# Weight units stored with their sums and loaded into the place of their smaller parts, operands prepared a chunk ahead, and a last chunk that hands its places over

## The chip, the cores and the metric

One core of one Trainium2 chip. Five engines work side by side and wait for each other through semaphores: TensorE (PE in the profile, its weight loads PEld), VectorE (DVE), ScalarE (ACT), GpSimd (POOL) and SyncE (SP), which here issues most of the DMAs. The metric is the device time of one execution in microseconds, the median of the runs. Everything is float32; each large product is made from a larger and a smaller part of each operand (`hi` and `lo`, in the format float32r), as three products of the parts.

## The reference

Random-feature attention over 8 batches of 8 heads with 576 positions of 64 values and 128 features, whose result, as 4608 rows of 512 values, goes through a gated layer of 1536 columns.

```python
def phi(x):
    proj = np.einsum('bhsd,md->bhsm', x, omega)
    h = proj - np.sum(x * x, axis=-1, keepdims=True) / 2.0
    h = h - np.max(h, axis=-1, keepdims=True)
    return np.exp(h) / np.sqrt(m)
q_p, k_p = phi(q * scale), phi(k * scale)
kv = np.einsum('bhsm,bhsd->bhmd', k_p, v)
num = np.einsum('bhsm,bhmd->bhsd', q_p, kv)
den = np.einsum('bhsm,bhm->bhs', q_p, np.sum(k_p, axis=2))[..., None] + 1e-06
x = (num / den).transpose(0, 2, 1, 3).reshape(4608, 512)
gate = 1.0 / (1.0 + np.exp(-(x @ w_gate)))
out = (gate * (x @ w_val)) @ w_out
```

The three weight matrices arrive as float64 and are converted on the chip.

## The kernel before

The work has four stages on TensorE.

1. **Attention**, in small steps (norms of rows `ss`, keys up to `kv`, queries up to `xs`), each with projections `pp`, maxima `mx`, exponentials, and for queries transposes `pt` and products `pn` and `px`. The finished columns `xs` go to the scratch `xT` in HBM. A generator interleaves the steps of several tasks.
2. **First pass**: four of the twelve column tiles of the gated layer, with plain products `gv` (line 225, 12 matmuls of 128x512 for gate and for value) over chunks of 512 rows of `xT`. A chunk's rows are loaded into `xr` and split into operands `xe` (ScalarE copies, GpSimd subtracts, line 70). Its results `ye` go to HBM. It starts as soon as the first rows of `xT` are there: one step of it, then fourteen small steps of attention (`RATE`), so that both share TensorE until attention ends; what remains of it then is its end.
3. **Second pass**: the other eight column tiles as four pairs, for nine chunks, by a scheme with 7 products in place of 8 (`gated`, products `gw`, line 320, 42 matmuls of 128x256 in each of 72 groups; a group belongs to a chunk, a pair and a kind, gate or value). Its results `yl` go to HBM.
4. **Third pass** (`last`, products `po`, line 416): for each of 18 half chunks 6 steps j of 21 matmuls with the output weights; its rows `yr` come back from `ye` and `yl` and are split into `yh` and `yl`.

Weights of the second and third pass form 14 units: 0 to 7 for the second, 8 to 13 for the third. Each comes as four blocks of 128x256 (1 MB as float64). A "piece" is half of it, 512 columns: `from_float64` takes six VectorE instructions (lines 78 to 94) and an add on GpSimd (line 96). The four converted blocks are kept in HBM (`w32`). Later `unit` loads them, makes four sums of blocks on VectorE (line 192) and splits the seven operands into a larger part (ScalarE, 128x768 and 128x1024) and a smaller part (VectorE). Eight units are converted beside attention, one piece every second step of the first pass (`PUT`), and six in the first pass's end.

A unit's parts lie in a place `u`, of which `late` has five and `tail` three. The pools: `early` holds the first pass's weights and closes with it; `a` is attention's and closes with attention; `late` opens then in the same memory; `tail` opens in place of `early`. Tiles of one tag share its places in turn, and an instruction that would overwrite a place waits for its last reader. In the last chunk units 8 to 13 are loaded through a single place, `xr` (named `wbt`).

A scheduler orders the instructions of each engine; those wrapped in `pin` keep the order in which they are written. Within an engine everything runs in order, so a waiting instruction holds up what stands behind it.

Of the kernel before, what the change touches and what calls it, by code (L numbers as in the profile page):

```python
# [48 lines left out]
PUT = 2  # L49
# [23 lines left out]
def from_float64(nc, both, bits, n):  # L73
# [3 lines left out]
    a, t = both[:, :n], both[:, n:]  # L77
# [19 lines left out]
    return x  # L97
# [3 lines left out]
def attn_glu_kernel(ctx: ExitStack, tc, qT, kT, qn, kn, va, om, ident, w, out):  # L101
# [6 lines left out]
    w32 = dram.tile([N_LATE, P, 4, Q], F32, name="w32")  # L108
# [30 lines left out]
    def piece(tiles, i):  # L139

        raw = tiles("wraw", i, 2 * WP).rearrange("p (n two) -> p n two", two=2)
        nc.sync.dma_start(out=raw, in_=w[:, i * WP : (i + 1) * WP, :])
        return from_float64(nc, tiles("f64", i, 2 * WP), raw, WP)

    def first_weights(pool, tiles):

        n = WE // WP
        for j in range(NE):
            ws[j] = wh, wl = [pool.tile([P, WE], F32R, name=f"{t}{j}") for t in ("wh", "wl")]
            for i in range(n):  # L150
                s = slice(i * WP, (i + 1) * WP)
                split(nc, wh[:, s], wl[:, s], piece(tiles, j * n + i), lo_engine=nc.gpsimd)
                yield

    def convert_weights(tiles, ns):

        flat = w32.rearrange("n p b q -> n p (b q)")
        k = 4 * Q // WP
        for n in ns:
            for i in range(k):  # L160
                x = piece(tiles, NE * WE // WP + n * k + i)
                nc.sync.dma_start(out=flat[n, :, i * WP : (i + 1) * WP], in_=x)
                yield

# [9 lines left out]
    def unit(pool, n, at=None):  # L174

        if at is None:
            both = keep.tile([P, KC, NC], F32, tag="xr", bufs=1, name=f"wbt{n}")
            b, t = both[:, :2], both[:, 2:]
        else:
            b, t = (buffer(f"{x}{n}", F32, at) for x in ("wb", "wt"))  # L180
        b, t = (x.rearrange("p a (b q) -> p (a b) q", q=Q) for x in (b, t))
        nc.sync.dma_start(out=b, in_=w32[n])
        yield
        u = pool.tile([P, 2, N_OPS, Q], F32R, tag="u", bufs=UL if pool is late else UE, name=f"u{n}")
        units[n] = u[:, 0], u[:, 1]
        for o, x, y in (
            (t[:, 0], b[:, 3], b[:, 0]),
            (t[:, 2], b[:, 2], b[:, 3]),
            (t[:, 1], b[:, 2], t[:, 0]),
            (t[:, 3], b[:, 1], t[:, 1]),  # L190
        ):
            nc.vector.tensor_tensor(out=o, in0=x, in1=y, op=ALU.subtract)
        split(nc, u[:, 0, :3], u[:, 1, :3], b[:, :3])
        split(nc, u[:, 0, 3:], u[:, 1, 3:], t)
        yield
# [10 lines left out]
    def first_pass():  # L206


        def parts_of(o, n):
            raw = load(o, n)  # L210
            yield
            for k in range(KC):
                x = buffer(f"xe{o}_{k}", at=keep)[:, :, :n]
# [17 lines left out]
        x = [t for t in parts_of(*chunks[0]) if t is not None]  # L231
        for (o, n), after in zip(chunks, chunks[1:] + [None]):
            ahead, parts = [], iter(())
            for j in range(NE):
                if j == NE - 1 and after:
                    parts = parts_of(*after)
                    next(parts)
# [4 lines left out]
                yield  # L242
                val = product(1, j, o, n, x)
# [7 lines left out]
            x = ahead + [t for t in parts if t is not None]  # L251
# [50 lines left out]
    def gated(c, x, pair, kind, g, y):  # L302
# [57 lines left out]
        pin(nc.sync.dma_start(out=yl[pair - EP, :, c], in_=y))  # L360

    def second_pass(x, parts):


        held = iter(())
        for c in range(NCH):
            ahead = None
            for pair in range(EP, NPAIR):
                g = keep.tile([P, 4, 2, P], F32, tag="g", bufs=2, name=f"gl{pair}_{c}")
                y = keep.tile([P, 2, N_OPS, P], F32, tag="y", bufs=2, name=f"yl{pair}_{c}")  # L370
                for kind in range(2):
# [12 lines left out]
                    yield c, pair  # L384
            x = ahead
        next(held, None)

    def last(c, s):
# [8 lines left out]
        for j in range(NPAIR):  # L397
            t, n = (("y", 2 * N_OPS), ("g", 8))[j % 2]
            raw = keep.tile([P, n, P], F32, tag=t, bufs=2, name=f"yr{id_}_{j}")[:, :8]
            if j < EP:  # L400
                nc.sync.dma_start(out=raw[:, :2], in_=ye[j, :, c, :, 0, s])
                nc.sync.dma_start(out=raw[:, 2], in_=ye[j, :, c, 1, 1, s])
                nc.sync.dma_start(out=raw[:, 7], in_=ye[j, :, c, 0, 1, s])
                for o, a, b, op in ((3, 7, 2, ALU.add), (4, 3, 0, ALU.subtract), (5, 0, 7, ALU.subtract), (6, 1, 4, ALU.subtract)):
                    nc.vector.tensor_tensor(out=raw[:, o], in0=raw[:, a], in1=raw[:, b], op=op)  # L405
            else:
                nc.sync.dma_start(out=raw[:, :N_OPS], in_=yl[j - EP, :, c, s])
# [95 lines left out]
    def keys(pool, u, p, b):  # L503
# [37 lines left out]
        kv = pool.tile([P, 2, E], F32, tag="kv", bufs=16, name=f"kv{u}_{p}_{b}")  # L541
# [4 lines left out]
    def queries(pool, u, p, b):  # L546
        for g in projected(pool, "q", u, p, b, qT):
# [54 lines left out]
            xs = pool.tile([P, nt * P], F32, tag="xs", bufs=XS, name=f"xs{id_}")  # L602
# [47 lines left out]
    keep = ctx.enter_context(tc.tile_pool(name="keep", bufs=1))  # L650
    with tc.tile_pool(name="early", bufs=1) as early:
        gates = first_pass()
        with tc.tile_pool(name="a", bufs=1, side="right") as pool:
            steps = attention(pool)

            def tiles(tag, i, n):
                return pool.tile([P, n], U32, tag=tag, bufs=2, name=f"{tag}{i}")
# [10 lines left out]
            later = convert_weights(tiles, range(UL + UE))  # L668
            n = credit = 0
            while not ready(B * S):  # L670
# [6 lines left out]
                if next(conv, conv) is conv and n % PUT == 0:  # L677
                    next(later, None)
# [3 lines left out]

        left = 2 * NE * (NCH + 1) - n

        def tiles(tag, i, n):
            return buffer(f"{tag}{i}", U32, late).rearrange("p a b -> p (a b)")

        conv = convert_weights(tiles, range(UL + UE, N_LATE))
        parts = iter(())
        for n, _ in enumerate(gates):  # L690
            if n < left - 2 * NE - 2:
                next(conv, None)
# [32 lines left out]
    for one in started:  # L725
        next(one)
# [76 lines left out]
```

## Time and profile before

| | |
|---|---|
| median of 3 runs | 1288.71 us (1285.23 to 1290.4) |
| the profiled execution's own time | 1282.94 us |
| its span | 1281.1 us |
| mean granted TensorE clock | 0.954 |
| TensorE busy in matmuls | 1176.0 us (92%) |
| VectorE busy | 904.7 us (71%) |
| attention and most of the first pass | 0 to 511.6 us |
| end of the first pass | to 584.4 us |
| second pass's products | 588.8 to 989.7 us |
| third pass | from 999.3 us to the end |

The profile's windows give, for a stretch of the span, the busy time of each engine and the number of its instructions, then TensorE's granted clock as a share of full speed and the busy share of the DMA engines. The waits give, for an engine and line, the time that it stood idle and the instruction that released it. The chain goes back from the last instruction through what released each. Instructions of tiles have the tile's name without its number; a line number is that of the kernel listed above.

### The profile page before, as it was taken

Reading aid. Unit: us, or ns where it says so; the run is one execution under the profiler, and the core shown is the slowest. Engines: PE = TensorE matmul, PEld = TensorE weight load, DVE = VectorE, ACT = ScalarE, POOL = GpSimd, SP = SyncE. Lnnn points to the kernel's source line nnn. Section 1 sums busy time; section 2 is a strip of 40 time slices with the busy share of each in tenths; the row PEclk is TensorE's granted clock in tenths of the full one; section 3 lists DMA queues with packets and bytes.
Section 4 is the critical chain, followed back from the end, with each engine's and each line's share of the span. In section 5 each row is a group of like instructions: output and inputs, shape, how many; then the busy total and the mean of one; then the engine's idle time right before and its main releaser. Section 6 shows DMA issues by size and latency. Waiting matters only on the chain.

```text
span 1281.1 us, 24183 instructions
## 1 busy us (share of the span) xinstructions
PE 1176.0 (92%) x8828; PEld 1110.7 (87%) x8828; DVE 904.7 (71%) x2057; ACT 604.7 (47%) x1222; POOL 496.8 (39%) x545
## 2 busy tenths in 40 slices
PE   5779989999999999883999999999996799999998
PEld 5768979788979888762899999999996799999998
DVE  7788988886676755778765665656656777777774
ACT  5557777778767674213422322223223444344331
POOL 3544452534142421332466666667643211111120
PEclk8869989999999999996999999999997799999999
DMA  7665778766534502675133233322333666666663
GB/s 260 209 192 161 213 230 269 222 210 185 177 93 119 165 32 90 194 227 171 63 143 110 98 120 138 131 109 98 120 120 124 204 204 205 200 188 190 182 185 104
DMA packets 104950, 206.58 MB, mean 161 GB/s; under 512 B 11136, under 2 KB 42112, under 8 KB 104832
## 3 DMA queue, kind: packets, MB, share of 16 engines
q1 hardware_dynamic: 87984, 186.09, 45.9%
q10 hardware_dynamic: 16848, 18.95, 4.3%
q8 instruction: 70, 1.15, 0.4%
q14 instruction: 48, 0.39, 0.1%
HBM read 136.31 MB, written 68.68 MB: 160 GB/s over the span
## 4 chain that ended last, share of the span: by engine, by line
PE 73%; DVE 13%; DMA 6%; issue 3%; ACT 2%; POOL 1%; SPq 1%; ACTq 0%; DVEq 0%; POOLq 0%
PE gw L320 26%; PE po L416 21%; PE gv L225 8%; PE pkv L537 5%; PE pnq L580 5%; PE ptq L568 2%; DMA wraw<-w 2%; DVE mxq L494 1%; DMA wbt<-w 1%; PE ppq L489 1%; DVE hq L557 1%; DVE mxk L494 1%; PE ppk L489 1%; PE pxq L597 1%; PE ppq L491 1%
## 5 line engine op out<-in xcount | busy, mean ns | idle before, releaser
L320 PE MATMUL gw<-xl,u 128*128 128x256 f32 x3024 | 373.2, 286 | 32.4 <-ACT p L331 19.6
L320 PEld LDWEIGHTS gw<-xl,u 128*128 128x128 f32 x3024 | 370.1, 194 | 35.7 <-ACT p L331 20.5
L416 PE MATMUL po<-u,yh 128*128 128x256 f32 x1512 | 273.6, 284 | 0.0
L416 PEld LDWEIGHTS po<-u,yh 128*128 128x128 f32 x1512 | 235.9, 191 | 0.0
L416 PE MATMUL po<-u,yl 128*128 128x256 f32 x756 | 214.7, 284 | 12.1 <-DVE yl L70 12.1
L225 PE MATMUL gv<-xe,wh 128*128 128x512 f32 (+1 forms) x640 | 198.9, 386 | 7.5 <-POOL xe L70 6.3
L69 ACT ACTIVATE yh<-yr 128x896 fp32r<-128x896 f32 x108 | 100.6, 950 | 162.3 <-PE po L416 72.8
L416 PEld LDWEIGHTS po<-u,yl 128*128 128x128 f32 x756 | 145.0, 192 | 12.5 <-issue 9.5
L225 PEld LDWEIGHTS gv<-xe,wh 128*128 128x128 f32 x640 | 115.8, 194 | 26.0 <-POOL xe L70 10.7
L225 PE MATMUL gv<-xe,wl 128*128 128x512 f32 (+1 forms) x320 | 124.4, 390 | 9.3 <-DVE ye L245 4.1
L70 POOL TENSOR_TENSOR yl<-yr,yh 128x896 fp32r<-128x896 f32 x18 | 41.1, 2281 | 221.9 <-PE po L416 151.9
L70 DVE TENSOR_TENSOR yl<-yr,yh 128x896 fp32r<-128x896 f32 x90 | 97.4, 1090 | 37.9 <-PE po L416 26.3
L70 POOL TENSOR_TENSOR loq<-rawq,hiq 128x256 fp32r<-128x256 f32 (+1 forms) x80 | 55.3, 704 | 126.2 <-ACT hiq L69 120.6
L300 DVE TENSOR_TENSOR u<-gw,p 128x256 f32<-128x256 f32 x144 | 60.7, 421 | 55.9 <-PE gw L320 47.8
L70 POOL TENSOR_TENSOR lok<-rawk,hik 128x256 fp32r<-128x256 f32 (+1 forms) x80 | 56.3, 714 | 103.1 <-ACT hik L69 100.3
L96 POOL TENSOR_TENSOR f<-f 128x512 f32<-128x512 f32 x36 | 48.3, 1340 | 102.5 <-DVE f L94 62.8
L405 DVE TENSOR_TENSOR yr<-yr 128x128 f32<-128x128 f32 x144 | 62.8, 468 | 30.1 <-DMA yr<-ye 29.5
L537 PE MATMUL pkv<-v,kpk 128*128 128x66 f32 x512 | 77.1, 285 | 3.7 <-ACT kpk L529 3.5
L225 PEld LDWEIGHTS gv<-xe,wl 128*128 128x128 f32 x320 | 61.8, 194 | 20.2 <-DVE ye L245 6.1
L580 PEld LDWEIGHTS pnq<-kv,qpq 128*128 128x128 f32 (+1 forms) x640 | 72.2, 192 | 7.6 <-ACT qpq L570 3.5
L537 PEld LDWEIGHTS pkv<-v,kpk 128*128 128x128 f32 x512 | 71.4, 204 | 7.5 <-ACT kpk L529 5.8
L529 ACT ACTIVATE kpk<-ppk,nbk 128x128 f32<-128x128 f32 x256 | 71.3, 384 | 11.6 <-DVE nbk L518 10.4
(103 smaller groups left out, 2226.9 us busy)
## 6 DMA issues: line engine op xcount, KB each, us to landing
yl<-yl SPq DMA_DIRECT2D x36, 896.0 KB, 3.8
yr<-yl SPq DMA_DIRECT2D x72, 448.0 KB, 3.8
wraw<-w SPq DMA_DIRECT2D x36, 512.0 KB, 4.5
xr<-xT SPq DMA_DIRECT2D x68, 256.0 KB, 4.5
v<-va SPq DMA_DIRECT2D x32, 330.0 KB, 3.5
natk<-kn SPq DMA_DIRECT2D x36, 256.0 KB, 3.8
natq<-qn SPq DMA_DIRECT2D x36, 256.0 KB, 3.5
out<-o ACTq DMA_DIRECT2D x36, 256.0 KB, 3.0
```

The costliest lines, as they stand in the source:

```text
L69: nc.scalar.activation(out=hi, in_=x, func=AF.Copy)
L70: (lo_engine or nc.vector).tensor_tensor(out=lo, in0=x, in1=hi.bitcast(F32), op=ALU.subtract)
L96: nc.gpsimd.tensor_tensor(out=x, in0=x, in1=r, op=ALU.add)
L225: nc.tensor.matmul(gv, lhsT=u[:, s], rhs=v, start=(m == 0), stop=(m == 3 * KC - 1))
L300: return nc.vector.tensor_tensor(out=o, in0=a, in1=b, op=ALU.add)
L320: nc.tensor.matmul(o, lhsT=u[:, k, s], rhs=v[:, kc, :], start=(first and m == 0), stop=(m == 5), skip_group_check=not first,)
L405: nc.vector.tensor_tensor(out=raw[:, o], in0=raw[:, a], in1=raw[:, b], op=op)
L416: nc.tensor.matmul(o, lhsT=u[:, i, :], rhs=v[:, k, :], start=(j + m == 0 and n in (1, 6, 5, 4)), stop=(j == NPAIR - 1 and m == 2), skip_gr ...
L489: nc.tensor.matmul(o, lhsT=lo[:, c], rhs=omH, start=True, stop=False)
L529: nc.scalar.activation(out=kp[t][:, h, :], in_=pp[:, 2 * i + h, :], func=AF.Exp, bias=nb[:, i, h : h + 1], scale=SCALE,)
L537: nc.tensor.matmul(pkv[:, h, :], lhsT=kp[b * MID + i][:, h, :], rhs=v[:, i, h, :], start=(i == 0), stop=(i == MID),)
L580: nc.tensor.matmul(pn[r, 2 * i + h, :], lhsT=qp[:, 2 * i + h, r], rhs=kvs[u, p, bb][:, h, :], start=True, stop=True,)
```

## The change

- `from_float64` writes to a place that it is given, with a scratch `a` that it is given. A unit's two halves are loaded at once into one tile `cv` of 7 times 512 columns (two such tiles take the place of the four smaller ones); the halves share one scratch. The first pass's weights are converted in the same way.
- The four sums are made when a unit is converted, and stored: `w32` holds eight blocks of a unit.
- `unit` loads the seven operands straight into the place of the smaller parts, in two DMAs; ScalarE copies the larger parts out, and the subtraction is done in place. In the last chunk the second subtraction goes to VectorE and GpSimd in turn, and all of it is pinned.
- Eleven units are converted beside attention (from step 14 on, two of every three steps), three in the first pass's end (`late0` to `late2`, in places of units).
- In the first pass's end the operands lie in two sets of buffers, `late` and `keep` in turn, so the next chunk is loaded and split while one is multiplied.
- Units 0 and 1 are loaded when `late` opens, 2 to 4 at the first pass's end, 5 to 7 at the second pass's start.
- Stores of `yl` are issued after the step that follows. In the last chunk each unit from 8 on is loaded into the place of the unit whose group has just ended. The third pass's first values (`yr`, j = 0 to 2) are read before the second pass has ended.
- `kv` has 15 places where it had 16, `xs` 2 where it had 3.

```diff
-def from_float64(nc, both, bits, n):
+def from_float64(nc, t, a, bits):
...
+    def converted(cv, i):
+        raw = [cv[:, (1 + h) * 2 * WP : (2 + h) * 2 * WP] for h in range(2)]
+        for h in range(2):
+            o = i + h * WP
+            nc.sync.dma_start(out=raw[h].rearrange("p (n two) -> p n two", two=2), in_=w[:, o : o + WP, :])
+        yield
+        for h in range(2):
+            from_float64(
+                nc, cv[:, h * WP : (h + 1) * WP], cv[:, 6 * WP :],
+                raw[h].rearrange("p (n two) -> p n two", two=2),
+            )
+            yield
...
     def convert_weights(tiles, ns):
         for n in ns:
+            cv = tiles(f"c{n}")
+            for _ in converted(cv, NE * WE + n * 4 * Q):
                 yield
+            f = cv[:, : 4 * WP].bitcast(F32).rearrange("p (b q) -> p b q", q=Q)
+            b, t = f[:, :4], f[:, 4:]
+            for o, x, y in (
...
+                nc.vector.tensor_tensor(out=o, in0=x, in1=y, op=ALU.subtract)
+            nc.sync.dma_start(out=w32[n], in_=f)
...
+    def unit(pool, n, lo_engine=None):
         u = pool.tile([P, 2, N_OPS, Q], F32R, tag="u", bufs=UL if pool is late else UE, name=f"u{n}")
...
+        whole = u[:, 1].bitcast(F32)
+        keep_order = pin if lo_engine else lambda x: x
+        keep_order(nc.sync.dma_start(out=whole[:, :3], in_=w32[n, :, :3]))
+        keep_order(nc.sync.dma_start(out=whole[:, 3:], in_=w32[n, :, 4:]))
+        yield
+        for o, engine in ((slice(0, 3), nc.vector), (slice(3, N_OPS), lo_engine or nc.vector)):
+            hi, lo, x = u[:, 0, o], u[:, 1, o], whole[:, o]
+            keep_order(nc.scalar.activation(out=hi, in_=x, func=AF.Copy))
+            keep_order(engine.tensor_tensor(out=lo, in0=x, in1=hi.bitcast(F32), op=ALU.subtract))
         yield
...
             for j in range(NE):
-                if j == NE - 1 and after:
-                    parts = parts_of(*after)
+                if after and parts is None and (j == NE - 1 or late):
+                    at = late if late and at is keep else keep
+                    parts = parts_of(*after, at)
                     next(parts)
...
+                if parts and at is late:
+                    ahead += [t for t in (next(parts, None),) if t]
...
-            later = convert_weights(tiles, range(UL + UE))
+            later = convert_weights(tiles, range(N_LATE - N_TAIL))
...
-                if next(conv, conv) is conv and n % PUT == 0:
+                if next(conv, conv) is conv and n >= FROM and n % 3:
                     next(later, None)
...
+        started = [unit(late, n) for n in range(2)]
+        for one in started:
+            next(one)
...
+        elif c == NCH - 1:
+            if 1 <= g <= NPAIR:
+                started.append(unit(late if g <= UL else tail, UL + UE + g - 1, (nc.vector, nc.gpsimd)[g % 2]))
+                next(started[-1])
+            if g >= 3:
+                next(started.pop(0))
+            if g == 3:
+                raws = [
+                    gated_values(0, 0, j, buffer(f"yr{j}", F32).rearrange("p a (b t) -> p (a b) t", t=P))
+                    for j in range(2)
+                ]
```

Where the order changes. First TensorE at attention's end (the last query tasks `3_7`, and `gv3072` of the first pass's chunk that begins at row 3072), before:

```order
L225 MATMUL gv3072_1_0_7498<-xe3072_0_7433,wl1_396 128x512
L225 MATMUL gv3072_1_0_7498<-xe3072_0_7433,wh1_395 128x512
L580 MATMUL pnq3_2_7_7303<-kv3_2_1_6750,qpq3_2_7_7286 128x66 x4
L568 MATMUL ptq3_3_7_7314<-id_sb_69,hq3_3_7_7301 128x128 x4
L225 MATMUL gv3072_1_0_7498<-xe3072_0_7433,wh1_395 128x512
L225 MATMUL gv3072_1_0_7498<-xe3072_1_7436,wl1_396 128x512
L225 MATMUL gv3072_1_0_7498<-xe3072_1_7436,wh1_395 128x512
L597 MATMUL pxq3_2_7_7321<-id_sb_69,xq3_2_7_7312 128x128 x2
```

and in the changed kernel:

```order
L613 MATMUL pnq3_2_7_7301<-kv3_2_1_6726,qpq3_2_7_7284 128x66 x4
L601 MATMUL ptq3_3_7_7312<-id_sb_69,hq3_3_7_7299 128x128 x4
L630 MATMUL pxq3_2_7_7319<-id_sb_69,xq3_2_7_7310 128x128 x2
L613 MATMUL pnq3_3_7_7325<-kv3_3_1_6768,qpq3_3_7_7317 128x66 x4
L630 MATMUL pxq3_3_7_7336<-id_sb_69,xq3_3_7_7334 128x128 x2
L236 MATMUL gv3072_0_0_7490<-xe3072_0_7455,wl0_112 128x512
L236 MATMUL gv3072_0_1_7512<-xe3072_0_7455,wl0_112 128x512
L236 MATMUL gv3072_0_0_7490<-xe3072_0_7455,wh0_111 128x512 x2
```

Attention's last steps have first-pass products between them before, and none now; chunk 3072 starts behind them. On ScalarE at that place, in the changed kernel:

```order
L636 ACTIVATE xsq3_3_7_7339<-pxq3_3_7_7336 128x256
L638 DMA xT_63<-xsq3_3_7_7339 128x256
L70 ACTIVATE xe3072_0_7455<-xr3072_0_7431 128x512
L70 ACTIVATE xe3072_1_7476<-xr3072_0_7431 128x512
L70 ACTIVATE xe3072_2_7479<-xr3072_0_7431 128x512
L70 ACTIVATE xe3072_3_7482<-xr3072_0_7431 128x512
L204 ACTIVATE u0_7405<-u0_7405 128x768
L255 ACT_TABLE_LOAD
L255 ACTIVATE ge3072_0_7503<-gv3072_0_0_7490 128x512
L204 ACTIVATE u0_7405<-u0_7405 128x1024
```

The copies of the chunk's operands, and the first copy of unit 0, now stand ahead of the first gate `ge`. Second, ScalarE at the second pass's start (`xl` its first operands, `p10` the first group's first sum, `u2` to `u5` copies of units), before:

```order
L262 ACTIVATE xl0_2_7989<-xr0_0_7865 128x512
L69 ACTIVATE u2_8011<-wt2_8009 128x1024
L69 ACTIVATE u3_8023<-wt3_8021 128x1024
L69 ACTIVATE u4_8035<-wb4_8032 128x768
L69 ACTIVATE u4_8035<-wt4_8033 128x1024
L331 ACTIVATE p10_2_0_8053<-gw0_0_2_0_8050 128x256
L69 ACTIVATE u5_8155<-wb5_8091 128x768
```

and in the changed kernel:

```order
L278 ACTIVATE xl0_2_7967<-xr0_0_7843 128x512
L347 ACTIVATE p10_2_0_8017<-gw0_0_2_0_8014 128x256
L356 ACTIVATE gl2_0_8012<-gw0_0_2_0_8014 128x256
L204 ACTIVATE u5_7999<-u5_7999 128x768
L347 ACTIVATE p11_2_0_8062<-gw0_1_2_0_8059 128x256
```

Four copies of units that stood ahead of the first `p10` are gone from there. Third, SP, which issues loads and stores, in the last chunk (`8` in `yl2_8` is the chunk), before:

```order
L182 DMA wbt10_12535<-w32_64 128x1024
L182 DMA wbt11_12602<-w32_64 128x1024
L401 DMA yr0_0_1_12815<-ye_65 128x2x128
L360 DMA yl_66<-yl4_8_12462 128x1792
L402 DMA yr0_0_1_12815<-ye_65 128x128
L403 DMA yr0_0_1_12815<-ye_65 128x128
L182 DMA wbt12_12678<-w32_64 128x1024
```

and in the changed kernel:

```order
L200 DMA u10_12401<-w32_64 128x1024
L422 DMA yr0_12408<-ye_65 128x2x128
L422 DMA yr0_12408<-ye_65 128x128 x2
L422 DMA yr1_12412<-ye_65 128x2x128
L422 DMA yr1_12412<-ye_65 128x128 x2
L386 DMA yl_66<-yl2_8_12154 128x1792
L199 DMA u11_12481<-w32_64 128x768
L200 DMA u11_12481<-w32_64 128x1024
L199 DMA u12_12544<-w32_64 128x768
L200 DMA u12_12544<-w32_64 128x1024
L424 DMA yr2_12551<-yl_66 128x896
L386 DMA yl_66<-yl3_8_12279 128x1792
```

The loads of units 11 and 12 and of the third pass's first values now stand ahead of the stores of pairs 3 and 4 of the last chunk.

More of the change, by code (lines that the diff above doesn't have):

```diff
@@ L250, in first_pass @@
                 yield
-            x = ahead + [t for t in parts if t is not None]
+            x = ahead + list(parts or ())
     def operands(c):
@@ L650, in attn_glu_kernel @@
     keep = ctx.enter_context(tc.tile_pool(name="keep", bufs=1))
+    late = None
+    stores = []
     with tc.tile_pool(name="early", bufs=1) as early:
@@ L697, in attn_glu_kernel @@
                 parts = operands(0)
                 x = next(parts)
-            else:
+            elif n > left - 2 * NE:
                 next(parts, None)
-        assert next(conv, conv) is conv
-        for n in range(2, UL):
-            for _ in unit(late, n, keep):
-                pass
+        assert not free and next(later, later) is later
+        started = [unit(late, n) for n in range(2, UL)]
+        for one in started:
+            next(one)
     tail = ctx.enter_context(tc.tile_pool(name="tail", bufs=1))
```

153 lines of the change are left out of this document (73 added, 80 removed).

## The prediction, made before the changed kernel was run

> **What bounds the kernel now.** I read the page's head first, then the span cut into stages, then the waits and the chain inside the poor stages.
>
> ```profile
> PE 1176.0 (92%) x8828; PEld 1110.7 (87%) x8828; DVE 904.7 (71%) x2057; ACT 604.7 (47%) x1222; POOL 496.8 (39%) x545
> PEclk8869989999999999996999999999997799999999
> PE 73%; DVE 13%; DMA 6%; issue 3%; ACT 2%; POOL 1%; SPq 1%; ACTq 0%; DVEq 0%; POOLq 0%
> ```
>
> TensorE is the bound, and its work is the same before and after: only its idle time and its slow-clock time can change. PEclk dips in slice 19 (the hand-over to the second pass) and slices 31 and 32 (the hand-over to the third). The stage tables (core's us, then busy time and instructions of PE, PEld, VectorE, ScalarE, GpSimd, then clock, DMA share, GB/s):
>
> ```profile
> 100.00:200.00 100.00, 90.67 (x720) 85.12 (x718) 87.58 (x247) 76.55 (x186) 45.87 (x54) 0.95 0.70 213
> 200.00:300.00 100.00, 96.77 (x673) 84.86 (x672) 83.09 (x231) 78.31 (x183) 37.04 (x42) 1.00 0.71 223
> 300.00:400.00 100.00, 96.29 (x697) 85.02 (x696) 69.06 (x198) 74.05 (x173) 34.19 (x44) 1.00 0.52 153
> 400.00:511.30 111.30, 110.44 (x791) 96.89 (x789) 68.00 (x199) 70.87 (x162) 30.02 (x38) 1.00 0.31 92
> ...
> 511.30:584.50 73.20, 63.36 (x257) 48.97 (x255) 56.12 (x88) 13.42 (x21) 26.27 (x19) 0.95 0.68 213
> 584.50:640.00 55.50, 33.37 (x237) 32.08 (x238) 44.84 (x82) 24.45 (x38) 19.92 (x19) 0.75 0.27 94
> 640.00:940.00 300.00, 300.00 (x2520) 300.00 (x2519) 182.94 (x392) 86.84 (x173) 195.62 (x233) 1.00 0.31 118
> 940.00:999.20 59.20, 39.87 (x272) 38.05 (x270) 39.05 (x79) 18.28 (x26) 22.16 (x27) 0.83 0.40 132
> 999.20:1020.00 20.80, 17.84 (x121) 17.67 (x122) 14.55 (x21) 8.62 (x10) 3.52 (x3) 0.83 0.68 211
> ```
>
> Prices of undisturbed TensorE work: the 640 to 940 row gives 300/2520 = 0.119 us for a second-pass product; for the third pass and the first:
>
> ```profile
> 1020.00:1260.00 240.00, 240.00 (x2013) 240.00 (x2013) 1.00 0.64 195
> 540.00:550.00 10.00, 10.00 (x46) 8.29 (x45) 7.08 (x13) 0.94 (x2) 2.99 (x3) 1.00 0.80 235
> ```
>
> That is 240/2013 = 0.1192 us and 10/46 = 0.217 us. Against them each poor stage loses: 511.3 to 584.5, 73.2 - 255 x 0.217 = 17.8 us; 584.5 to 640, 55.5 - 237 x 0.119 = 27.3; 940 to 999.2, 59.2 - 272 x 0.119 = 26.8; 999.2 to 1020, 20.8 - 121 x 0.1192 = 6.4. Together 78 us; the two hand-overs hold 60.5 of them. What ended TensorE's waits there (us in total, times, longest), by stage, and last what held up SP, which issues loads and stores, from 940 to 1020:
>
> ```profile
> PE gv L225 <- POOL xe L70: 5.7, 4, 3.1
> PE gv L225 <- DVE ye L245: 4.0, 3, 1.7
> ...
> PE gw L320 <- ACT p L331: 14.1, 2, 13.0
> ...
> PE po L416 <- DVE yl L70: 12.1, 2, 9.3
> PE gw L320 <- ACT p L331: 5.4, 2, 4.2
> PE gw L320 <- DVE u L300: 4.7, 5, 3.2
> ...
> SPq L360 <- POOL yl L359: 25.9, 4, 12.8
> ```
>
> The engines named are only the last link. Behind them stand loads of unit blocks, as the chain (start, us, what) and ScalarE's timeline show:
>
> ```profile
> 512.02 2.46 DMA xT<-xsq
> ...
> 601.10 5.25 DMA wb<-w
> ...
> 953.38 5.46 DMA wbt<-w
> ...
> 967.04 5.48 DMA wbt<-w
> ...
> 1276.49 0.42 DVE u2o L300
> ```
>
> ```profile
> 608.71 1.06 ACT L69 ACTIVATE u<-wt 128x1024 fp32r<-128x1024 f32 x1 [1.49 <-DVE wt L192]
> 609.67 0.37 ACT L331 ACTIVATE p<-gw 128x256 f32<-128x256 f32 x1
> ```
>
> ScalarE runs in order, so the first `p` of the second pass stands behind the copies of unit 4, whose blocks were issued at 601.10. That is the 13.0 us wait. In the last chunk every unit goes through one place (`wbt`), 13.7 us from one load to the next (953.38 to 967.04), while a pair of groups lasts 84 x 0.119 = 10 us.
>
> **The change part by part.** *Second pass's start.* The units are loaded with their sums, 0 and 1 as soon as `late` opens, 2 to 4 inside the first pass's end; in the new order no copy of units 0 to 4 stands behind the last `xl`, and the first `p` follows it directly. Units 5 to 7 can be loaded only when `early` closes, at the second pass's start; the first five groups, 5 x 42 x 0.119 = 25 us, don't need them, and a load of 5.3 us with copies and lows is ready in less than half of that. Queued behind those copies on ScalarE is the second group's `p`: a wait of 0 to 6 us (one load; a gain is excluded, as nothing can run before its operands). I take 3 where 27.3 were: 24 us gained.
>
> *Second to third pass.* Units 8 to 13 go one by one into the places of units whose groups are done (each load is released at a group's end, every 5 us), with no sums, and the first chunk's values are read early. Per unit VectorE pays at most these two lows, and GpSimd takes half of the larger ones:
>
> ```profile
> L70 DVE TENSOR_TENSOR u<-wb,u 128x768 fp32r<-128x768 f32 x8 | 7.7, 968 | 0.0
> L70 DVE TENSOR_TENSOR u<-wt,u 128x1024 fp32r<-128x1024 f32 x8 | 10.8, 1353 | 2.6 <-ACT u L69 2.6
> L192 DVE TENSOR_TENSOR wt<-wb 128x256 f32<-128x256 f32 x16 | 7.6, 502 | 0.9 <-DMA wb<-w 0.9
> L192 DVE TENSOR_TENSOR wt<-wb,wt 128x256 f32<-128x256 f32 x16 | 7.2, 448 | 0.0
> L96 POOL TENSOR_TENSOR f<-f 128x512 f32<-128x512 f32 x12 | 15.9, 1326 | 52.1 <-DVE f L94 41.1 <-issue 8.2 <-DMA w<-f 2.8
> ```
>
> A 917 KB load is 1.75 times the 512 KB one, and the reads of the fourth value set stand behind a `yl` store on SP, which waits for GpSimd's products (25.9 us in four such waits now). Unit 13 is released with group 6 and copied on ScalarE ahead of the third pass's `yh` of j = 3. No row shows this arrangement. Lower bound: 3 us, the last two groups' tail of `yl` on GpSimd. Upper: 14, a load, a split and a store behind each other (5.5 + 3 + 5.5). I take 8, the middle, where 26.8 + 6.4 = 33.2 were: 25 us gained.
>
> *First pass's end.* Half the conversions leave it (6 pieces in place of 12), but 24 products remain after attention where 21.25 (255/12) did, since the new order has products further ahead early and none between attention's last steps: 288 x 0.217 = 62.6 us. Stalls: the first product waits for `xe` copies that now stand behind attention's last `xsq` on ScalarE, and goes at GpSimd's pace (about 4 us); then `ge` stands among the copies of unit 0, which load only after attention's last store; the conversions still hold VectorE ahead of `ye`, with the shared scratch added (8); the rest 3. Bounds: 5 us (the `xe` start alone) and 25 (the old 17.8, and a late load of 7 in front of `ge`). I take 15. Operands prepared a chunk ahead cost nothing while ScalarE is 13.4 of 73 us busy; without that cover they cost what they did, 5.7 us.
>
> *Attention stage.* Three more units and 44 sums go to VectorE. A piece by the tile's own busy time:
>
> ```profile
> 100.00:200.00 100.00, 31.20 (x52) 0.00 (x0) 12.23 (x9) 0.95 0.70 213
> ```
>
> 52 instructions are 8.67 pieces of six, 3.6 us each. So 6 x 3.6 + 44 x 0.475 = 42 us more, and by the new order conversions run on to about 425 us, 11 units of 9.1 us over 328 us: 30 us per 100. On 300 to 400 that makes 69 + 30 = 99% of VectorE. While it ran at 83% (200 to 300) TensorE lost 3.2 us, no more than at 69% (3.7); at 88% it lost 9.3. Lower bound 0. Upper: what is over 88% has to be done later, 11 x 1.25 = 14 us. I take 5, because TensorE has first-pass products 9 to 11 us further ahead to fill with, and VectorE falls back to 61% after 425.
>
> Here the port between VectorE and GpSimd matters. The same instruction takes two times:
>
> ```profile
> 100.65 1.38 DVE L85 TENSOR_SCALAR f<-f 128x512 uint32<-128x512 uint32 x1
> ...
> 110.82 0.42 DVE L85 TENSOR_SCALAR f<-f 128x512 uint32<-128x512 uint32 x1
> ```
>
> The Trainium skill, page "SBUF — State Buffer", section "Who interferes with whom", says that VectorE's fast mode, and (its rules at the end add) an operation of two SBUF inputs, excludes GpSimd for the whole instruction and the later of the two waits. The trace agrees as far as 1.38 against 0.42 goes. By that rule, the added sums, which have two SBUF inputs, would each wait in the 37% of the time in which GpSimd works: an estimate of 44 x 0.37 x 0.96 = 16 us more on VectorE, and a sum of 1258 to 1262 in place of mine if 11 to 15 of them reach TensorE. It speaks for the first rival below.
>
> *Others.* Stores of units grow from 512 KB to 1 MB, 11 over 328 us at a DMA share of 0.5 to 0.7: hidden. Fewer `kv` and `xs` places: no wait of the trace names them.
>
> **The sum**, in the profiled execution's time (span 1281.1, own time 1282.94, the median of the three runs 1288.71, which is 0.45% more): attention's end, now 511.6 (the last `xT` store of the chain starts at 512.02), goes to 516.6; + 62.6 + 15 = 594.2; + 3024 x 0.119 (72 groups of 42) + 3 = 957; + 8 + 2268 x 0.1192 (18 x 6 x 21) = 1235.4; + 4.6 from the last sums to the end, as now (1276.49 to 1281.1) = 1240; + 1.8 outside the span = 1242; x 1.0045 = 1247 us.
>
> **The rivals.**
> *VectorE becomes the bound in attention, or the last hand-over stays tight.* Attention's end then moves 14 to 20 us instead of 5, or DMA (six units of 0.92 MB, four stores of 0.92 and 2.3 MB of reads, 11.5 MB in some 45 us, 255 GB/s, where no stage above passes 235) holds the third pass by 20 instead of 8. For: 99% above. Against: 83% cost nothing. Time 1256 to 1270, about 1262.
> *All is hidden.* Attention ends when it did (for: 200 to 300), the first pass's end loses 5, the hand-over 3: 5 + 10 + 5 + 2 less, 1225. Against: `xe` behind `xsq`, and VectorE ahead of `ye`.
> *Slower.* Both halves of a unit share the scratch `a`, so the second half's first VectorE instruction waits for GpSimd's add of the first (1.33 us itself), and everything on in-order VectorE, `mx` and `h` of attention too, queues behind. There are 4 + 14 such waits. It decides at 48 / 18 = 2.7 us of exposed stall each on top of my sum: then 1296 or more. Against: in all but two or three places 1 to 36 other VectorE instructions stand between the two, and GpSimd is only 37% busy.
>
> **How the numbers follow.** My forecast 0.58, its own range 1232 to 1262; the first rival 0.22; all hidden 0.14; slower 0.04; the rest, 0.02, no change. From 1222 to 1270 reaches into both neighbours. A change of this kernel can be told from none at about 0.5%, 6.4 us, as the three runs lie 5.2 apart. Faster 0.94, same 0.02, slower 0.04.
>
> **What would show it.** Right: no wait of TensorE over 4 us named `p` after the second pass's start; no `wbt`; in the third's start waits of under 10 us in all; the last `xsq` at 513 to 522; VectorE over 90% in 300 to 400 with TensorE still over 93. Wrong: TensorE's share in 100 to 425 falls by more than 3 points, or VectorE's first instruction of a half (L78) shows waits on GpSimd of 2 us and more, or the first pass ends past 610.

## The result: 1.1% faster, a third of the forecast

The changed kernel takes 1273.72 us (median of 4 runs, 1270.91 to 1276.31) against 1288.2 us for the kernel before (4 runs): ratio 0.9889, 95% interval 0.9859 to 0.9919. Forecast were 1247 us, with a range of 1232 to 1262 of its own and of 1222 to 1270 with parts of the neighbouring cases. The direction was right, but 14.5 us came in place of 42, and the time lies outside both ranges, beyond the first rival too (1256 to 1270). The profiled execution took 1272.84 us, with a span of 1271.0.

The page's head after (busy time of the engines, granted clock, shares of the chain):

```profile
PE 1180.4 (93%) x8828; PEld 1115.5 (88%) x8828; DVE 900.3 (71%) x2054; ACT 600.5 (47%) x1220; POOL 505.9 (40%) x548
PEclk8768889999999999599999999999999999999999
PE 71%; DVE 12%; POOL 5%; DMA 5%; issue 4%; ACT 3%; SPq 1%; ACTq 0%; DVEq 0%; POOLq 0%
```

The two dips of the clock at the hand-overs are gone (slices 19 and 31, 32 of before), and there is one of 0.5 in slice 17, about 508 to 540 us, where none was. The first slices are lower too. The windows of after, columns as in the prediction:

```profile
100.00:200.00 100.00, 87.22 (x663) 83.47 (x662) 83.05 (x235) 73.57 (x178) 44.03 (x50) 0.88 0.60 200
200.00:300.00 100.00, 95.39 (x668) 83.57 (x667) 90.09 (x247) 76.94 (x171) 36.62 (x43) 1.00 0.73 241
300.00:400.00 100.00, 98.19 (x680) 85.88 (x679) 87.30 (x239) 75.29 (x170) 41.03 (x45) 1.00 0.62 213
...
560.00:580.00 20.00, 13.90 (x55) 10.39 (x55) 19.37 (x32) 5.84 (x9) 11.50 (x8) 0.97 0.59 190
580.00:600.00 20.00, 18.02 (x74) 14.28 (x74) 9.91 (x17) 4.35 (x8) 2.20 (x1) 0.94 0.82 277
600.00:620.00 20.00, 20.00 (x95) 16.45 (x94) 10.84 (x16) 7.34 (x12) 3.87 (x3) 1.00 0.17 61
620.00:640.00 20.00, 16.64 (x134) 16.02 (x134) 14.11 (x24) 8.55 (x13) 6.27 (x6) 1.00 0.60 196
640.00:940.00 300.00, 300.00 (x2519) 300.00 (x2518) 182.36 (x391) 88.01 (x174) 196.34 (x235) 1.00 0.31 118
...
960.00:980.00 20.00, 18.23 (x150) 17.80 (x149) 17.15 (x31) 10.38 (x16) 12.07 (x11) 1.00 0.89 294
980.00:1000.00 20.00, 16.83 (x136) 16.21 (x135) 17.96 (x20) 8.65 (x11) 16.84 (x14) 1.00 0.43 135
1000.00:1020.00 20.00, 15.67 (x118) 15.25 (x117) 10.44 (x23) 6.71 (x8) 4.18 (x2) 0.91 0.78 242
```

Both hand-overs gained nearly what was forecast. The first pass's last product starts at 617.9 us and ends at 618.3; 600 to 640 lost 5 us. From 960 to 1020, 60 - 404 x 0.1192 = 11.8 us are lost where 33.2 were. From the end of the first pass (584.4 before, 618.3 after) to the end of the span it is 696.7 us before and 652.7 after: 44 gained. But the first pass ends 33.9 us later. One place stands out, the 40 us from 500 to 540, first of before, then of after:

```profile
500.00:540.00 40.00, 36.41 (x171) 28.97 (x170) 25.52 (x44) 12.88 (x20) 11.76 (x9) 0.96 0.55 171
```

```profile
500.00:540.00 40.00, 28.26 (x135) 24.07 (x135) 14.34 (x46) 9.09 (x20) 4.35 (x4) 0.63 0.16 50
```

135 matmuls in place of 171, mostly small ones of attention, at a clock of 0.63. TensorE's timeline there, at attention's end:

```profile
527.97 1.12 PE L601 MATMUL ptq<-id_sb,hq 128*128 128x128 f32 x4 [1.52 <-DVE hq L590]
528.88 0.64 PE L630 MATMUL pxq<-id_sb,xq 128*128 128x128 f32 x2
529.77 1.97 PE L613 MATMUL pnq<-kv,qpq 128*128 128x66 f32 x8 [0.26 <-ACT qpq L603]
532.76 0.66 PE L630 MATMUL pxq<-id_sb,xq 128*128 128x128 f32 x2 [1.02 <-DVE xq L624]
536.35 1.22 PE L236 MATMUL gv<-xe,wl 128*128 128x512 f32 x2 [2.94 <-ACT xe L70]
```

Attention's steps wait for each other there, with nothing between them: between 496.0 and 536.4 us no first-pass product starts. In the kernel before, the longest such stretch from 470 us to attention's end is 3.2 us. The chain (start, us, what) shows what the next first-pass product waits for:

```profile
533.46 0.39 ACT xsq L636
...
533.87 1.70 DMA xT<-xsq
...
535.67 0.64 ACT xe L70
...
536.38 5.00 POOL xe L71 x4
```

The copies `xe` of chunk 3072 begin when attention's last store has landed, which is when pool `a` closes. The diff says why: `at = late if late and at is keep else keep` puts the first chunk prepared after attention's code, 3072, into `late`, and `late` lies in the memory of `a`.

To compare stages I count TensorE's work: matmuls of each shape times about the spacing of back-to-back ones (0.217 us for 512 columns, 0.113 for 256, 0.110 for 128, 0.105 for 66). By it the changed kernel is behind by 10.5 us at 200 us, 10.8 at 500, 28.1 at 540, and at the first pass's end by the 33.9 us that it comes later. So there are three losses: before 200 us, from 500 to 540 (17), and some 6 behind. From 200 to 500, with VectorE at 87 to 90% until 400, nothing was lost.

One thing has to be known before single traces are compared. Nine traces (the changed kernel's and eight of its variants in the experiments) have the same instructions in the same order on TensorE, VectorE, ScalarE and GpSimd up to 300 us, and yet their work by 200 us goes from 109 to 115 us. So where a few us decide, two traces are compared below from a point up to which their order is the same, and the lag at that point is taken off.

### The profile page after: what moved, and what is told of

The parts are those of the page before. It is cut to its first block, busy times and chain, and to the rows that moved or that the text cites. A ratio compares the mean times of both kernels' runs of the same rounds, so it can differ in the third digit from the quotient of the medians.

```text
span 1271.0 us, 24153 instructions
## 1 busy us (share of the span) xinstructions
PE 1180.4 (93%) x8828; PEld 1115.5 (88%) x8828; DVE 900.3 (71%) x2054; ACT 600.5 (47%) x1220; POOL 505.9 (40%) x548
## 4 chain that ended last, share of the span: by engine, by line
PE 71%; DVE 12%; POOL 5%; DMA 5%; issue 4%; ACT 3%; SPq 1%; ACTq 0%; DVEq 0%; POOLq 0%
PE gw L336 25%; PE po L449 20%; PE gv L236 9%; PE pnq L613 4%; PE pkv L570 4%; PE ptq L601 2%; DMA u<-w 1%; POOL xe L71 1%; DVE mxk L527 1%; DVE mxq L527 1%; DVE hq L590 1%; PE ppq L522 1%; DMA natk<-kn 1%; PE ppq L524 1%; PE ppq L523 1%
## 5 line engine op out<-in xcount | busy, mean ns | idle before, releaser
L336 PE MATMUL gw<-xl,u 128*128 128x256 f32 x3024 | 362.8, 282 | 7.0 <-DVE u L316 6.8
L336 PEld LDWEIGHTS gw<-xl,u 128*128 128x128 f32 x3024 | 361.2, 190 | 8.6 <-DVE u L316 8.0
L71 POOL TENSOR_TENSOR yl<-yr,yh 128x896 fp32r<-128x896 f32 x18 | 39.6, 2199 | 214.7 <-PE po L449 114.6
L440 DVE TENSOR_TENSOR yr<-yr 128x128 f32<-128x128 f32 x144 | 66.1, 493 | 48.7 <-DMA yr<-ye 48.3
L71 POOL TENSOR_TENSOR loq<-rawq,hiq 128x256 fp32r<-128x256 f32 (+1 forms) x80 | 57.9, 736 | 98.7 <-ACT hiq L70 90.5
L613 PEld LDWEIGHTS pnq<-kv,qpq 128*128 128x128 f32 (+1 forms) x640 | 75.9, 200 | 11.3 <-ACT qpq L603 8.3
L236 PEld LDWEIGHTS gv<-xe,wl 128*128 128x128 f32 x320 | 62.6, 197 | 25.9 <-DVE ye L261 10.8
L613 PE MATMUL pnq<-kv,qpq 128*128 128x66 f32 (+1 forms) x640 | 79.7, 284 | 4.5 <-ACT qpq L603 4.4
```

What stands on the lines that cost most here:

```text
L71: (lo_engine or nc.vector).tensor_tensor(out=lo, in0=x, in1=hi.bitcast(F32), op=ALU.subtract)
L236: nc.tensor.matmul(gv, lhsT=u[:, s], rhs=v, start=(m == 0), stop=(m == 3 * KC - 1))
L336: nc.tensor.matmul(o, lhsT=u[:, k, s], rhs=v[:, kc, :], start=(first and m == 0), stop=(m == 5), skip_group_check=not first,)
L613: nc.tensor.matmul(pn[r, 2 * i + h, :], lhsT=qp[:, 2 * i + h, r], rhs=kvs[u, p, bb][:, h, :], start=True, stop=True,)
```

## The experiments

All are timed against the kernel before on the same chip, which differs from experiment to experiment. Ratios are to it, with 95% intervals.

**Chunk 3072 in `keep`**

```diff
-                    at = late if late and at is keep else keep
+                    at = late if late and at is keep and after[0] != 6 * NC else keep
```

> The changed kernel, but the operands of the first pass's chunk 3072 stay in keep, as before the change; the later chunks alternate as changed. Theory F (filler): chunk 3072's operands lie in the late pool, which opens only when attention's pool closes, so attention's last steps have no first-pass products between them. It expects the last xsq at 510 to 517 us instead of 533.5, about 19 products left behind it, the first pass's end at 585 to 597 instead of 618, and a time of 1240 to 1254 us (1273.7 now). Rival V (VectorE's 42 us of added work set attention's end): last xsq stays at 528 or later, time 1266 or more.

Measured: 1251.48 us, 0.9717 (0.9679 to 0.9755): 22 us less than the changed kernel. The last `xsq` (first and last start) seems not to have moved, and the window 500 to 540 is now full:

```profile
L636 ACT ACTIVATE xsq<-pxq x80: 257/383/411, 52.2 to 535.1; 128x256 f32<-128x256 f32 x64, 128x128 f32<-128x128 f32 x16
```

```profile
500.00:540.00 40.00, 39.80 (x262) 34.20 (x261) 21.98 (x63) 22.72 (x39) 8.57 (x9) 1.00 0.24 79
```

But this trace is of the slowest of the four runs (1257.63 us), and at 450 us, where the order is still that of the changed kernel, it is 7.7 us behind it. With this taken off the last `xsq` comes at 527.4 us instead of 533.5, and the first pass ends at 595.6 instead of 618.3. The four other traces of this order (the one with a scratch of its own, and three of the paced kernel) agree: last `xsq` at 527.4 or 527.5 with their lags taken off. In the first of the paced kernel, as it stands:

```profile
L636 ACT ACTIVATE xsq<-pxq x80: 259/384/412, 52.3 to 524.4; 128x256 f32<-128x256 f32 x64, 128x128 f32<-128x128 f32 x16
```

So the time is as the filler theory said, and the mechanism mostly: the first pass runs beside attention's last steps, whose longest stretch without first-pass products is 5.2 us now. Attention itself ends 6 us sooner, not the 16 or more that the theory expected. What remained was one long wait, and the VectorE work in front of it in the chain:

```profile
PE gv L236 <- DVE ye L261: 11.6, 2, 11.0
```

```profile
561.98 1.74 DVE late L81 x2
563.72 4.20 DVE late L180 x3
567.92 1.40 DVE late L85
...
572.47 0.61 DVE ye L261
```

**Units 8 to 10 not converted beside attention** (the changed kernel; unit 7's values are stored in their places)

```diff
+            if 8 <= n < N_LATE - N_TAIL:
+                yield
+                yield
+                yield
+                continue
...
-            nc.sync.dma_start(out=w32[n], in_=f)
+            for m in (n,) if n != 7 else (7, 8, 9, 10):
+                nc.sync.dma_start(out=w32[m], in_=f)
```

> The changed kernel, with the conversions and sums of units 8 to 10 left out beside attention (unit 7's values are stored in their places, so the output is not the reference's): 27 us less work for VectorE, about all that the change added there but for 15 us. F: the last xsq stays within 3 us of 533.5, time within 5 us of 1273.7. V: the last xsq at 520 or earlier, time 1250 to 1262.

Measured: 1259.91 us, 0.9778 (0.975 to 0.9806), last `xsq` at 518.0 us. The numbers are those of rival V, so my theory alone was too simple. But the stretch without filler is gone here as well, though chunk 3072 still lies in `late`: first-pass products of the chunk ahead now last until 515.3 us, and the longest stretch without them is 5.6 us (40.4 in the changed kernel).

```profile
500.00:540.00 40.00, 34.76 (x179) 27.69 (x178) 22.80 (x45) 18.71 (x29) 9.37 (x8) 0.91 0.47 169
```

I read this so: with the added conversions attention falls behind the first pass, whose products then run out before attention ends; without 27 us of them they last. The run does not show a cost of VectorE's load apart from the emptied stretch.

**Both together**

> The first and second experiment together: chunk 3072's operands in keep, and units 8 to 10 not converted beside attention (wrong values in their places). If VectorE's load costs time only where TensorE has nothing between attention's last steps: last xsq earlier (515 to 525) but the time within 4 us of the first experiment's 1251.5. If VectorE's load costs TensorE time in any case: 1238 to 1244 us.

Measured: 1250.91 us, 0.9705 (0.9685 to 0.9725), the first experiment's time within 0.6 us, with the last `xsq` at 521.3. All of its runs (1247.98 to 1252.81) lie above the 1238 to 1244 of the other expectation. So the two are one loss, the emptied stretch, and each edit fills it. With first-pass products between attention's steps, leaving out VectorE's added work brought nothing that these runs show; without them it brought 14 us.

**The misplacement alone, in the kernel before**

```diff
-                x = buffer(f"xe{o}_{k}", at=keep)[:, :, :n]
+                x = buffer(f"xe{o}_{k}", at=late if o == 6 * NC else keep)[:, :, :n]
```

> The kernel before, with one edit: the operands of chunk 3072 lie in late, as the change puts them. Nothing else is added, VectorE's work is that of before. F: the last xsq moves from 511.6 to 525 to 537, the first pass's end by 15 to 32 us, and the time to 1302 to 1320 us. V: the last xsq within 3 us of 511.6, time within 6 us of 1288.

Measured: 1301.39 us, 1.0099 (1.0066 to 1.0132). The last `xsq` came at 514.4, as V said, but the last of the first pass's products starts 31 us later than before (584.0), as F said:

```profile
L225 PE MATMUL gv<-xe,wh x640: 278/392/796, 78.9 to 614.8; 128*128 128x512 f32 x128, 128*128 128x256 f32 x32
```

The total rose by only 11 us, because part of the old stall at the second pass's start now ran beside the late products (by 640 us the second pass was 15 us behind the kernel before). The edit shows a loss from the place alone, without any added VectorE work. Its size is not that of the changed kernel, though. Attention's last 18.8 us have no first-pass products here (40.4 there), and right behind them TensorE waits 12.3 us for `xe` of the same chunk, as GpSimd's first `xe` starts at 529.16 us, behind adds of conversions:

```profile
PE gv L225 <- POOL xe L70: 14.9, 3, 12.3
```

**A scratch of its own for the late units** (the first experiment's kernel; a second half's scratch in one of `late`'s buffers)

> The first experiment's kernel, with a scratch of its own for the second half of each of the three units that are converted in the first pass's end. If VectorE's waits for GpSimd's add hold up ye there: 3 to 6 us less than the first experiment, and no wait of L78 for L96 behind attention. If those waits are hidden: within 2 us of the first experiment.

Measured: 1262.49 us, 0.9798 (0.9765 to 0.9831), 11 us more than the first experiment; neither expectation held. TensorE's waits show a new one:

```profile
PE gv L237 <- DVE ye L262: 8.2, 2, 6.1
PE gv L237 <- POOL xe L71: 7.9, 2, 6.8
```

Freed from the scratch, two of the conversions' adds stand behind each other on GpSimd ahead of the `xe` subtractions, which start at 555.45 us behind adds that began at 550.35. It looks as if the scratch's wait had been of use, as it spread the conversions out; no run tests this apart.

**The late conversions paced** (the first experiment's kernel)

```diff
-            else:
+            elif n % 2 == 0:
                 next(later, None)
```

> The first experiment's kernel, in which the three units of the first pass's end are converted in steps at every second step of the first pass instead of every one. There TensorE waited 11.0 us once for ye, whose VectorE instruction stood behind some 20 us of conversions. If this queueing is the cause: that wait falls under 4 us and the time is 5 to 11 us less than the first experiment's 1251.5. If the conversions are needed earlier (units 2 to 4 late): a new wait at the second pass's start, time the same or more.

Measured: 1241.61 us, 0.9635 (0.9614 to 0.9656), 10 us less than the first experiment. The longest wait for `ye` fell from 11.0 to 2.4 us, and all waits for it from 11.6 to 5.2:

```profile
PE gv L236 <- DVE ye L261: 5.2, 3, 2.4
```

Run again later beside other variants it took 1244.57 us, 0.9644 (0.961 to 0.9679), which is 7 us less than the first experiment:

> The paced kernel once more, beside the two on the same chip: 1239 to 1246 us, from its runs of 1239.4 to 1244.0.

A third set of runs (below, conversions from step 24 on, which gave the same program) took 1246.04 us. In the traces, with the lag at 450 us taken off, the first pass ends at 589.1, 589.4 and 589.6 us, where the first experiment has 595.6. So pacing is worth 6 us there, which is what the waits for `ye` lost; the rest of the 10 lies within the scatter. This is the version that beats both kernels, by 3.2 to 3.6% the kernel before and by 2.2 to 2.5% the changed one.

**The loss before 200 us.** Six kernels looked for it and none found it. Two edits of the kernel before, fewer places (`kv` 15, `xs` 2) and one scratch for all conversions beside attention:

```diff
-        kv = pool.tile([P, 2, E], F32, tag="kv", bufs=16, name=f"kv{u}_{p}_{b}")
+        kv = pool.tile([P, 2, E], F32, tag="kv", bufs=15, name=f"kv{u}_{p}_{b}")
...
-    a, t = both[:, :n], both[:, n:]
+    a, t = both[:, :n] if a is None else a, both[:, n:]
```

> The kernel before with 15 places for kv and 2 for xs, as the change has them, and nothing else. The changed kernel has done 10.5 us less TensorE work by 200 us. If the places are the cause: TensorE's work by 200 us falls by 7 us or more, and the time rises by 6 to 12 us. If not: within 3 us of the kernel before.

> The kernel before in which all conversions beside attention share one scratch, so that each piece's first VectorE instruction waits for GpSimd's add of the piece before (24 pieces; in the changed kernel every second one). If this wait is what costs the first 200 us: TensorE's work by 200 us falls by 7 us or more, the time rises by 6 to 15 us. If VectorE finds the add done: within 3 us of the kernel before.

Measured: 1285.96 us, 0.9979 (0.9948 to 1.0009), and 1301.32 us, 1.0097 (1.008 to 1.0114). By 200 us TensorE's work was 118.7 and 113.3 us, where the kernel before had 123.3 and the changed one 112.7. The first falls by 4.6 us, no more than traces of one order differ; the second by 10. The scratch looked like the cause. Taking it out of the changed kernel, with pacing and without:

```diff
-                nc, cv[:, h * WP : (h + 1) * WP], cv[:, 6 * WP :],
+                nc, cv[:, h * WP : (h + 1) * WP], cv[:, 2 * WP : 3 * WP] if h else cv[:, 6 * WP :],
```

> The paced kernel, in which a unit's second half takes as scratch the place of the first half's raw bits, which only VectorE reads and has done with, so that no VectorE instruction waits for GpSimd's add there. Scratch theory: in the kernel before, a shared scratch cost 10.4 us of TensorE's work by 200 us and 12.8 us in all, with 23 such waits; with 18 of them 6 to 12 us come back: 1230 to 1236 us, TensorE's work by 200 us up by 5 to 10 us. Rival (order: both halves loaded at once and other tiles set the order of the first 200 us): within 3 us of 1241.6.

> The changed kernel with that scratch alone. Scratch theory: 6 to 12 us less than 1273.7, so 1262 to 1268. Rival: within 3 us of 1273.7, or, if attention that runs further ahead only lengthens its stretch without first-pass products, the same though TensorE's work by 200 us rises.

Measured: 1249.28 us, 0.9703 (0.9671 to 0.9735), no gain on the paced kernel, and 1275.85 us, 0.9896 (0.9873 to 0.9919), as the changed kernel. VectorE's waits on the second half (4.3 us in all) were gone, yet the work by 200 us was 114.1 and 114.6 us. The scratch theory falls for the changed kernel. Then the places given back, and the conversions begun at step 4 or 24 of the first pass instead of 14:

> The paced kernel with 16 places for kv and 3 for xs again (room for them comes from the scratch: a first half uses the second half's place, a second half that of the first half's raw bits). If the fewer places cost the first 200 us: TensorE's work by 200 us up by 5 to 10 us (115.0 in the paced kernel, 123.3 in the kernel before) and 1232 to 1237 us. If not: within 4 us of the paced kernel.

> The paced kernel with the units' conversions from step 4 of the first pass on instead of step 14, so that they begin where they began in the kernel before. If the later start (conversions meeting a denser stretch of attention) is the cause: TensorE's work by 200 us up by 5 us or more, time down by as much. If conversions anywhere cost the same: within 4 us of the paced kernel, or slower by up to 8, as more of them fall into the start, where TensorE has no first-pass products beside them.

> The paced kernel with the units' conversions from step 24 of the first pass on instead of 14. If the conversions themselves hold up the first 200 us: TensorE's work by 200 us up from 115 to 120 or more, and what is saved is lost again after 400 us, where they then go on to attention's end: time 1240 to 1255. If the first weights' conversions and the order of attention's start are the cause, work by 200 us stays at 113 to 117.

Measured: 1256.39 us, 0.9734 (0.9705 to 0.9764); 1254.08, 0.9719 (0.9681 to 0.9758); 1246.04, 0.9685 (0.9655 to 0.9714). By 200 us: 114.0, 114.8 and 111.9. The first two lost 8 to 10 us more than the paced kernel from 300 to 400, where the first experiment, with the paced kernel's order, lost 5 more. The last one tests nothing: all its instructions stand in the same order as with step 14, so it is the paced kernel run a third time, and 111.9 against 115 is scatter.

**Units 8 to 13 loaded only after the second pass** (the changed kernel, last chunk)

```diff
-            if 1 <= g <= NPAIR:
-                started.append(unit(...))
-                next(started[-1])
-            if g >= 3:
-                next(started.pop(0))
...
         if c == NCH:
+            for h in range(1, NPAIR + 1):
+                started.append(unit(...))
+                next(started[-1])
```

> The changed kernel, but units 8 to 13 are loaded only when the second pass is done, all at once, each into the place that the change gives it; the first values of the third pass are read early as changed. If the hand-over of places in the last chunk is what brought the second to third pass's loss from 33.2 to about 11.6 us: a loss of 25 to 40 there, time 1287 to 1302. If most of that gain came from the stored sums and the early values: within 6 us of 1273.7.

Measured: 1280.34 us, 0.9928 (0.9903 to 0.9953), 6.6 more than the changed kernel; 960 to 1040 lost 18.6 us there, 11.7 in the changed kernel. The totals of the two traces differ by 12.4 us, but 5.4 of them lie before the first pass's end, where the order is the same. Neither expectation was right, the second just missed: passing places on early brings 7 of the 21 us. What brings the other 14 was not taken apart; the stored sums, the removed single place and the early first values are left for it.

## Why the prediction was wrong, point by point

| step | predicted | measured |
|---|---|---|
| attention's end (last `xT` store) | 516.6 us | 533.9 |
| from there to the first pass's end, over 62.6 us of products | 15 | 21.8 |
| loss at the second pass's start | 3 | 5 |
| loss at the second hand-over | 8 | 11.8 |
| span | 1240 | 1271.0 |

- **The step that failed** is the attention stage's "I take 5, because TensorE has first-pass products 9 to 11 us further ahead to fill with". At the end it had none. I had seen in the order that no products stand between attention's last steps, and counted it only as 24 products instead of 21.25 left over. That TensorE would stand idle or at a lower clock for some 20 us between dependent steps, I did not price. From 500 to 540 it cost 17 us; the first experiment gave back 22 in all. One of my own signs of being wrong came with it: the first pass ended past 610 us.
- **VectorE at its limit**, the first rival, was the right worry with the wrong place. At 87 to 90% busy it cost TensorE nothing (90.09 busy beside 95.39 of TensorE at 200 to 300, and 87.30 beside 98.19 at 300 to 400, where I had counted 99). It cost 14 us only by letting the filler run out. The estimate worked out by the Trainium skill, page "SBUF — State Buffer", section "Who interferes with whom" (16 us more on VectorE, or 0.36 us for each added sum), does not agree with the trace: the 44 sums beside attention took 480 ns each on average and 417 in the median, so such waits are nearer 0.06 us each, 3 us in all.

```profile
L180 DVE TENSOR_TENSOR c<-c 128x256 f32<-128x256 f32 x44 | 20.5, 480 | 6.2 <-POOL c L96 6.2
```

  The rival's other half, that DMA holds the third pass, did not come either: 11.8 us were lost there, with 294 GB/s in 960 to 980, where I had seen no more than 235 before.
- **The scratch**, the mechanism of the slower rival, was no cause of what was lost in the changed kernel, although one scratch shared by all pieces cost the kernel before 1%.
- **The first pass's end** was mis-sized by 7 us, and not in the "8" for VectorE's conversions ahead of `ye`, of which TensorE's waits from 540 to 618 us show 8.5:

```profile
PE gv L236 <- DVE ye L261: 8.5, 5, 2.3
```

  Some 3 us are the price of a product. The row 540 to 550 counts 46 matmuls, but two of them started before it; 10/44 is 0.227 us, and 288 products are 65.4 us, not 62.6. Most of the rest are products at less than full pace, beside a granted clock of 0.50 until 540 us and 0.94 to 0.97 from 540 to 600.
- **The loss before 200 us**, 10.5 us, was in none of my terms. My bound for attention looked at 300 to 400 us. It is real, as all nine traces of the changed order (109 to 115 us of work) lie below the kernel before (123.3), and from 100 to 200 the granted clock is 0.88 in place of 0.95. Its cause stays open: not the scratch, and neither the places nor a start at step 4 moved it by more than the scatter. The order of the whole stage is another one, and most edits made a new one.
- **The hand-overs** went by their mechanism: no wait of TensorE for `p` of more than 4 us, no single place, and 22 and 21 us gained where 24 and 25 were forecast. The rest of the span's error, under 2 us, was not looked for.

## What to carry to other kernels

When buffers move to a pool that opens later, ask which work was overlapping the old pool's end and can now not start; the filler it was may be worth more than the stall that is removed. Look in the order for stretches in which an engine has only one chain of dependent steps, and price their latency, not their work. In this case VectorE near 90% was harmless while TensorE had other work, so test an added load and a lost filler together before blaming either, and look in the traces whether an edit that lightens the load has also changed the filler. Before reading a difference of a few us between two traces, compare two traces of the same order: here they differ by up to 6 us of work at 200 us.

## What was not expected of the hardware

TensorE's clock fell even where no wait was long: from 500 to 540 us the waits shown were 0.3 to 2.9 us each, and the granted clock was 0.63. Matmuls of 256 columns follow each other there at 0.12 us (509.5 to 510.6) or at 0.21 us (519.0 to 520.1), a full and about a half pace. The Trainium skill, page "TensorE: Matmul & The Clock Gate", section "A second HAM failure mode: psum-queue depth-cycling", tells of a kernel in which frequent short idling between groups of matmuls makes the clock gate swing between half and full. The trace agrees with such a swing: TensorE was busy 28 of the 40 us, and no wait shown there was long. But the share of busy time does not give the clock by itself. From 520 to 540 us TensorE was busy 13.02 of 20 us at 0.50; from 560 to 580, with first-pass products, 13.90 of 20 at 0.97:

```profile
520.00:540.00 20.00, 13.02 (x47) 9.82 (x46) 4.83 (x15) 4.97 (x11) 3.62 (x3) 0.50 0.22 71
560.00:580.00 20.00, 13.90 (x55) 10.39 (x55) 19.37 (x32) 5.84 (x9) 11.50 (x8) 0.97 0.59 190
```

What makes the difference, the kind of matmul or how the waits lie, no run here separates.
